# Banded attention of batches 2 and 3 in whole runs beside a channel mix, and a reordered last expert

## The chip, the cores and the metric

The kernel runs on one core of a Trainium2 chip. The metric is the device time of one execution in microseconds (us), the median of three runs. TensorE is called PE below, its weight loads PEld; VectorE is DVE, ScalarE is ACT, GpSimd is POOL, and SyncE (SP) issues most of the DMAs. Each engine works through its own list of instructions in order; a scheduler writes these lists when the kernel is built, from the order in which the code is written and from its priorities.

## The reference

Three layers on a batch of 4, sequence S = 576, width 512, all in float32:

```
q, k, v: (4, 8, 576, 64)                       # 8 heads of 64
1. banded attention: scores = q @ k.T / 8
   heads 0-3: 0 <= i-j < 32;  heads 4-7: 0 <= i-j < 128 and (i-j) % 4 == 0;  else -1e9
   x = softmax(scores) @ v                      -> (4, 576, 512)
2. channel mix: x_prev = x shifted by one row
   xk = mu_k*x + (1-mu_k)*x_prev;  xr = mu_r*x + (1-mu_r)*x_prev
   y = sigmoid(xr @ w_r) * (relu(xk @ w_k)**2 @ w_v)     # w_k 512x1024, w_v 1024x512
3. mixture of 4 attention experts: the gate picks the top 2 of y @ w_gate, with softmax weights
   out = sum over chosen e of weight_e * causal_attention_e(y) @ wo[e]   # head width 64
```

## The kernel before, in words

**Channel mix.** It is computed in half sequences of 288 columns. Every large product is made of three fp32r products (`product`, line 521): the high half of the weight with the high half of the data, high with low, and low with high. The halves of the data come from `mix`: ACT rounds the mixed data `m` to its high half `xh` (line 510), and POOL subtracts it to leave the low half `xl` (line 511). `receptance` makes `z`, `keys` makes `h` and splits its square into `kh` and `kl` (line 545, on DVE, for batch 1 on POOL for every second block), and `values_of` makes `v`. All these products use the whole 128 x 128 array.

**Banded attention.** Heads are taken in pairs, four pairs a batch. For each pair `attn_weights` makes scores for nine blocks of 64 queries, in two score buffers of five and four blocks; in each block the two heads (`j` = 0, 1) sit on two 64 x 64 tiles of the array (line 303). For batches 2 and 3 DVE and ACT then make the weights, DVE turns them in 32 x 32 squares (`turn_weights`), they go out to DRAM and come back as `pT`, and `attn_values` multiplies them by the values (line 377), again two small products per block. The attention of batch b+1 is issued beside the channel mix of batch b: `attn_batch` (batch 1) and `attn_later` (batches 2 and 3) are generators that a loop at the end advances together with the channel mix. From the written order the scheduler chooses, product by product, what PE does next.

**Expert attention.** For each batch and each pair of experts g, `queries_keys` makes `pq` and `pk`, splits them into `qh`, `ql`, `kh`, `kl` (lines 814 to 817, one buffer of each), and SP copies these into the operands `qs`, `kk`, `kl2` of the scores (line 823). `values` makes `pv` and the gate. `scores` (lines 910, 912) makes the causal scores of one expert in five blocks of queries and normalises them, `context` transposes the weights (`pt`, line 957), copies them (`wt`) and makes the value sums (`av`, lines 983, 988) of two experts together, and `project` makes the output (`po`, line 1020). A table `plan` says which generators go side by side with which expert, and in how many steps.

Of the kernel before, what the change touches and what calls it, by code (L numbers as in the profile page):

```python
# [21 lines left out]
def tile_dilated_attention__rwkv_channel_mix__moe_attention(  # L22
# [20 lines left out]
    DM = 512  # L43
# [237 lines left out]
    def attn_weights(ap, b, hp, qT, kT):  # L281
# [7 lines left out]
        def products(t0, t1):  # L289
# [67 lines left out]
    def attn_values(ap, b, hp, vw, pe=None, pT=None):  # L357
# [4 lines left out]
        for i in range(3):  # L362
# [69 lines left out]
    def attn_later(ap, first):  # L432
# [10 lines left out]
        for n, (b, hp) in enumerate(pairs):  # L443
# [9 lines left out]
            next(weights)  # L453
            if behind:
# [3 lines left out]
            yield  # L458
# [55 lines left out]
    def product(o, wts, xs, kts, wsl):  # L514
# [16 lines left out]
    def keys(dp, b, c, fo, kh, kl, xk, wts):  # L531
# [12 lines left out]
        half = nc.gpsimd if b == 1 and fo % 2 == 0 else nc.vector  # L544
# [191 lines left out]
    with s2:  # L736
# [61 lines left out]
        def queries_keys(b, g):  # L798
# [3 lines left out]
            ql = ep.tile([128, S], F32R, tag="ql", name=f"ql_{b}_{g}", bufs=1)  # L802
            kh = ep.tile([128, S], F32R, tag="kh", name=f"kh_{b}_{g}", bufs=1)
            qh = ep.tile([128, S], F32R, tag="qh", name=f"qh_{b}_{g}", bufs=1)
            kl = ep.tile([128, S], F32R, tag="kl", name=f"kl_{b}_{g}", bufs=1)
# [88 lines left out]
        def scores(b, e):  # L894
# [7 lines left out]
            for t, (t0, tn) in enumerate(TB):  # L902
# [3 lines left out]
                for i, (c0, c1) in enumerate(parts):  # L906
# [5 lines left out]
                    nc.tensor.matmul(sc, qs[g][:, e % 2, t0 : t0 + 128], kl2[g][:, e % 2, c0:c1],  # L912
                                     start=False, stop=True)
# [12 lines left out]
            nc.vector.tensor_scalar_add(st[:, 2, :], st[:, 2, :], 1e-9)  # L926
            nc.vector.reciprocal(st[:, 3, :], st[:, 2, :])
            assert ("v", b) in emitted
            nc.vector.tensor_mul(st[:, 3, :], st[:, 3, :], gt[:, :, e])
            for t, (t0, tn) in enumerate(TB):  # L930
                n = t0 + tn
                tn = 128
                pb = pe[:tn, PO[t] : PO[t] + n]
                if t == NB - 1:
                    nc.scalar.activation(pb, pb, AF.Copy, scale=st[:tn, 3, t : t + 1])
                else:
                    nc.vector.tensor_scalar_mul(pb, pb, st[:tn, 3, t : t + 1])
            weights[(b, e)] = pe
            yield
# [3 lines left out]
        def context(b, e):  # L943
# [5 lines left out]
            heads[e % 2] = []  # L949
            moved = []  # L950
            for i, grp in enumerate(groups):
                pt = ps("pt", f"pt2_{nm}_{i}")
                for kb, t in grp:
                    k0, kn = TB[kb]
                    tn = 128
                    c0 = place(kb, t)[1]
                    nc.tensor.transpose(pt[:kn, c0 : c0 + tn], pe[:tn, PO[t] + k0 : PO[t] + k0 + kn], ident[:tn, :tn])  # L957
                wt = ep.tile([128, 512], F32, tag="wt", name=f"wt{i}_{nm}", bufs=10)
                heads[e % 2].append(wt)
                for rows, c0, c1 in regions[i]:  # L960
                    if ("aava", "avav")[e % 2][i] == "a":
# [3 lines left out]
                yield  # L965
            if e % 2 == 0:
                return
            av1 = ps("av", f"av1_{nm}")
            av0 = ps("pt", f"av0_{nm}")
            two = [(64 * x, heads[x], vt[:, :, 64 * (2 * g + x) : 64 * (2 * g + x) + 64]) for x in range(2)]  # L970

            def after_all(ins):

                if kb == 0:
                    for m in moved:
                        tc.add_manual_dep(ins.ins, m.ins.name, together, reason="both experts' products together")

            for kb in range(NB):
                k0, kn = TB[kb]
                i, c0 = place(kb, max(kb, 1))  # L980
                q0 = max(k0, 64)
                for p0, w, vh in two:
                    ins = nc.tensor.matmul(av1[p0 : p0 + 64, q0 - 64 : 512], vh[:kn, kb, :], w[i][:kn, c0 : c0 + S - q0],  # L983
                                           start=(kb == 0), stop=(kb == NB - 1))
                    after_all(ins)
                if kb == 0:
                    for p0, w, vh in two:
# [121 lines left out]
```

## Time and profile before

| what | value |
|---|---|
| time, median of 3 runs | 571.47 us (571.39 to 571.98) |
| the profiled execution's own time, its span | 570.95 us, 569.2 us |
| PE busy | 548.3 us, 96% of the span |
| DVE, ACT, POOL busy | 349.9, 333.8, 64.8 us |
| granted TensorE clock, mean | 0.991 of full speed |
| 0 to 60 us | banded attention of batch 0, loading and splitting of the weights |
| 60 to 367 us | channel mix of batches 0 to 3, banded attention of batches 1 to 3 beside it |
| 367 to 569 us | expert attention |

How to read it: PE is busy nearly always, so the time is a sum of what PE does one after another, plus the stretches at the start, inside the expert attention and at the end in which it waits. A PE matmul's shown length includes the time in the pipeline, in which the next one already runs. What one costs is therefore the distance from its start to the next one's start. An fp32 product of the banded attention leaves two records in the trace, an fp32r product one.

### The profile page before, as it was taken

Reading aid. Unit: us, or ns where it says so; the run is one execution under the profiler, and the core shown is the slowest. Engines: PE = TensorE matmul, PEld = TensorE weight load, DVE = VectorE, ACT = ScalarE, POOL = GpSimd, SP = SyncE. Lnnn points to the kernel's source line nnn. Section 1 sums busy time; section 2 is a strip of 40 time slices with the busy share of each in tenths; the row PEclk is TensorE's granted clock in tenths of the full one; section 3 lists DMA queues with packets and bytes.
Section 4 is the critical chain, followed back from the end, with each engine's and each line's share of the span. In section 5 each row is a group of like instructions: output and inputs, shape, how many; then the busy total and the mean of one; then the engine's idle time right before and its main releaser. Section 6 shows DMA issues by size and latency. Waiting matters only on the chain.

```text
span 569.2 us, 12508 instructions
## 1 busy us (share of the span) xinstructions
PE 548.3 (96%) x4669; PEld 490.5 (86%) x4669; DVE 349.9 (61%) x1145; ACT 333.8 (59%) x940; POOL 64.8 (11%) x89
## 2 busy tenths in 40 slices
PE   9978989999999999999999999999998999999985
PEld 4757989989889999999999999999986988988663
DVE  3788989665889268356361526438667549565652
ACT  3789998655877075455253625227575757655851
POOL 8400000001123032110022303000000000000000
PEclk9997999999999999999999999999999999999998
DMA  9968296857676124120100320054504615506202
GB/s 165 244 209 244 85 243 126 146 100 164 136 162 147 43 60 119 40 52 27 38 1 1 83 67 1 2 126 115 137 23 103 171 30 126 139 24 181 76 0 94
DMA packets 130173, 57.66 MB, mean 101 GB/s; under 512 B 109928, under 2 KB 117184, under 8 KB 130112
## 3 DMA queue, kind: packets, MB, share of 16 engines
q1 hardware_dynamic: 129680, 56.41, 42.0%
q8 instruction: 37, 0.61, 0.5%
q0 software_dynamic: 416, 0.44, 0.4%
q14 instruction: 24, 0.20, 0.1%
q10 hardware_dynamic: 16, 0.00, 0.0%
HBM read 34.42 MB, written 10.03 MB: 78 GB/s over the span
## 4 chain that ended last, share of the span: by engine, by line
PE 81%; DVE 7%; ACT 5%; DMA 3%; SPq 2%; issue 1%; DVEq 0%; ACTq 0%
PE v L521 19%; PE h L521 14%; PE z L521 7%; PE pv L836 5%; PE sc L303 5%; PE av L983 5%; PE av L377 4%; PE po L1020 4%; PE pt L957 4%; PE pq L521 3%; PE pk L521 3%; PE idle L76 2%; PE sc L910 2%; PE sc L912 2%; SPq L189 2%; PE pt L367 2%
## 5 line engine op out<-in xcount | busy, mean ns | idle before, releaser
L521 PE MATMUL h<-xh,wk_hi 128*128 128x288 f32 x256 | 77.5, 304 | 1.8 <-ACT r L535 1.7
L521 PE MATMUL h<-xl,wk_hi 128*128 128x288 f32 x256 | 75.7, 296 | 0.6 <-DVE xl L500 0.6
L521 PE MATMUL v<-kh,wv_hi 128*128 128x288 f32 x256 | 75.7, 301 | 0.0
L521 PE MATMUL h<-xh,wk_lo 128*128 128x288 f32 x256 | 75.2, 294 | 0.0
L521 PE MATMUL v<-kl,wv_hi 128*128 128x288 f32 x256 | 75.1, 297 | 0.0
L521 PE MATMUL v<-kh,wv_lo 128*128 128x288 f32 x256 | 74.5, 295 | 0.0
L922 ACT ACTIVATE pe<-pe,st 128x64 f32<-128x64 f32 (+4 forms) x80 | 44.9, 562 | 19.2 <-DVE st L916 18.8
L535 ACT ACTIVATE r<-h 128x288 f32<-128x288 f32 x64 | 26.0, 410 | 48.6 <-PE h L521 42.4
L521 PEld LDWEIGHTS h<-xh,wk_hi 128*128 128x128 f32 x256 | 47.8, 187 | 4.5 <-ACT r L535 2.9
L511 POOL TENSOR_TENSOR xl<-m,xh 128x1152 fp32r<-128x1152 f32 x12 | 32.4, 2700 | 167.1 <-ACT xh L510 86.5
L916 DVE CUSTOM_DVE_ANT_0 pe<-sc,cmask 128x64 f32<-128x64 f32 (+4 forms) x80 | 33.6, 425 | 25.9 <-PE sc L912 25.7
L521 PEld LDWEIGHTS h<-xl,wk_hi 128*128 128x128 f32 x256 | 48.1, 188 | 0.9 <-DVE xl L500 0.8
L521 PEld LDWEIGHTS v<-kh,wv_hi 128*128 128x128 f32 x256 | 47.6, 187 | 1.2 <-DVE r L542 0.2
L521 PEld LDWEIGHTS h<-xh,wk_lo 128*128 128x128 f32 x256 | 48.2, 188 | 0.0
L521 PEld LDWEIGHTS v<-kh,wv_lo 128*128 128x128 f32 x256 | 47.9, 188 | 0.3
L521 PEld LDWEIGHTS v<-kl,wv_hi 128*128 128x128 f32 x256 | 47.9, 188 | 0.3
L327 ACT ACTIVATE pe<-pe,st 128x96 f32<-128x96 f32 x108 | 39.1, 365 | 13.4 <-DVE st L322 13.2
L497 DVE SCALAR_TENSOR_TENSOR m<-x,mus,m 128x288 f32<-128x288 f32 x64 | 29.9, 507 | 26.1 <-ACT m L496 26.1
L521 PE MATMUL z<-xh,wr_hi 128*128 128x288 f32 x128 | 39.8, 314 | 0.7 <-ACT z L529 0.7
L551 DVE SCALAR_TENSOR_TENSOR x<-z,v 128x288 f32<-128x288 f32 x32 | 14.3, 453 | 40.4 <-PE v L521 40.3
L521 PE MATMUL z<-xl,wr_hi 128*128 128x288 f32 x128 | 38.7, 303 | 0.0
L521 PE MATMUL z<-xh,wr_lo 128*128 128x288 f32 x128 | 38.2, 300 | 0.0
(183 smaller groups left out, 1439.2 us busy)
## 6 DMA issues: line engine op xcount, KB each, us to landing
kk<-kh SPq DMA_DIRECT2D x32, 144.0 KB, 2.7
kl<-kl SPq DMA_DIRECT2D x32, 144.0 KB, 2.6
raw_in_moe_w_k_dram<-in_moe_w_k_dram SPq DMA_DIRECT2D x4, 1024.0 KB, 7.5
raw_in_moe_w_v_dram<-in_moe_w_v_dram SPq DMA_DIRECT2D x4, 1024.0 KB, 6.4
out_dram<-ob SPq DMA_DIRECT2D x16, 256.0 KB, 3.1
rqk<-in_q_dram SPq DMA_DIRECT2D x48, 72.0 KB, 2.5
rqk<-in_k_dram SPq DMA_DIRECT2D x48, 72.0 KB, 2.5
moved<-turned SPq DMA_DIRECT2D x8, 432.0 KB, 2.9
```

The source lines that it names most:

```text
L303: nc.tensor.matmul(sc[h, c0 : c0 + WK], qT[h, QB * t : QB * t + QB], kT[h, k0 : k0 + WK], start=(b > 0), stop=(b > 0 or t == t1 - 1))
L327: nc.scalar.activation(pe[:, t, :], pe[:, t, :] if b else sc[:, c0 : c0 + WK], AF.Exp, bias=st[:, 0, t : t + 1], scale=-1.0, accum_out=st[ ...
L377: nc.tensor.matmul(av[64 * j : 64 * j + 64, p0 % 288 : p0 % 288 + u1 - u0], vw[:, j, t, :], (pts[:, 128 * a + 64 * j + u0 : 128 * a + 64 * ...
L497: nc.vector.scalar_tensor_tensor(out=m, in0=x, scalar=mus[:, 0, w, f : f + 1], in1=m, op0=ALU.mult, op1=ALU.add)
L511: nc.gpsimd.tensor_sub(lo, m, hi.bitcast(F32))
L521: nc.tensor.matmul(o, w[:, kt, wsl], x[:, kt, :], start=(n == 0), stop=(n == last))
L535: nc.scalar.activation(r, p, AF.Relu)
L836: nc.tensor.matmul(p, x[:, kt, t0 : t0 + tn], w[:, kt, 512:772], start=(n == 0), stop=(n == 3 * KT - 1))
L916: nc.vector.tensor_tensor_reduce(out=pe[:tn, PO[t] + c0 : PO[t] + c1], in0=sc, in1=m, scale=-0.125, scalar=(BIG if i == 0 else st[:tn, 1, ...
L922: nc.scalar.activation(pb, pb, AF.Exp, bias=st[:tn, 0, t : t + 1], scale=-1.0, accum_out=st[:tn, 2, t : t + 1])
L957: nc.tensor.transpose(pt[:kn, c0 : c0 + tn], pe[:tn, PO[t] + k0 : PO[t] + k0 + kn], ident[:tn, :tn])
L983: ins = nc.tensor.matmul(av1[p0 : p0 + 64, q0 - 64 : 512], vh[:kn, kb, :], w[i][:kn, c0 : c0 + S - q0], start=(kb == 0), stop=(kb == NB - 1))
```

## The change

It has five parts. (1) For batches 2 and 3 each couple of banded products (both heads of a block) is told to come after the latest channel-mix product that the code has issued so far (`together_with`). (2) In `mix` the high and low half are made in two pieces, of two of the four features each. (3) In batch 1 the low half of the seventh block of keys is made by DVE instead of POOL. (4) `ql`, `kh`, `qh`, `kl` have two buffers. (5) The last expert of the last batch has an order of its own: its scores are made from the last block of queries to the first and normalised in two groups, its weights are transposed in five groups, its value sums are made for the later 256 columns first, the last projection is split by g, three projections of batch 2 are held back to chosen places (`fill`), two of the last outputs are issued by ACT, and the last rows of the plan are other.

```diff
                 c0 = WK * (t - t0)
-                for j in range(2):
-                    h = slice(64 * j, 64 * j + 64)
-                    nc.tensor.matmul(sc[h, c0 : c0 + WK], qT[h, QB * t : QB * t + QB], kT[h, k0 : k0 + WK],
-                                     start=(b > 0), stop=(b > 0 or t == t1 - 1))
+                with together_with(b, 2):
+                    for j in range(2):
+                        h = slice(64 * j, 64 * j + 64)
+                        nc.tensor.matmul(sc[h, c0 : c0 + WK], qT[h, QB * t : QB * t + QB], kT[h, k0 : k0 + WK],
+                                         start=(b > 0), stop=(b > 0 or t == t1 - 1))
...
-                    for j in range(2):
-                        nc.tensor.matmul(
-                            av[64 * j : 64 * j + 64, p0 % 288 : p0 % 288 + u1 - u0],
-                            vw[:, j, t, :],
-                            (pts[:, 128 * a + 64 * j + u0 : 128 * a + 64 * j + u1] if pT is None
-                             else pT[:, 2 * j + u0 // 32 : 2 * j + u1 // 32, t, :]),
-                            start=True, stop=True,
-                        )
+                    with together_with(b, 2):
+                        for j in range(2):
+                            nc.tensor.matmul(
+                                av[64 * j : 64 * j + 64, p0 % 288 : p0 % 288 + u1 - u0],
+                                vw[:, j, t, :],
+                                (pts[:, 128 * a + 64 * j + u0 : 128 * a + 64 * j + u1] if pT is None
+                                 else pT[:, 2 * j + u0 // 32 : 2 * j + u1 // 32, t, :]),
+                                start=True, stop=True,
+                            )
...
         if b:
-            nc.scalar.copy(hi, m)
-            nc.gpsimd.tensor_sub(lo, m, hi.bitcast(F32))
+            for f in (slice(0, KT // 2), slice(KT // 2, KT)):
+                nc.scalar.copy(hi[:, f], m[:, f])
+                nc.gpsimd.tensor_sub(lo[:, f], m[:, f], hi[:, f].bitcast(F32))
...
-                nc.tensor.matmul(o, w[:, kt, wsl], x[:, kt, :], start=(n == 0), stop=(n == last))
+                marks["product"] = nc.tensor.matmul(o, w[:, kt, wsl], x[:, kt, :], start=(n == 0), stop=(n == last)).ins
...
+    def together_with(b, first):
...
+        return tc.issue_after(marks["product"]) if b >= first and "product" in marks else ExitStack()
...
-        half = nc.gpsimd if b == 1 and fo % 2 == 0 else nc.vector
+        half = nc.gpsimd if b == 1 and fo % 2 == 0 and fo < FT - 2 else nc.vector
...
-            ql = ep.tile([128, S], F32R, tag="ql", name=f"ql_{b}_{g}", bufs=1)
-            kh = ep.tile([128, S], F32R, tag="kh", name=f"kh_{b}_{g}", bufs=1)
...
+            ql = ep.tile([128, S], F32R, tag="ql", name=f"ql_{b}_{g}", bufs=2)
+            kh = ep.tile([128, S], F32R, tag="kh", name=f"kh_{b}_{g}", bufs=2)
...
-            for t, (t0, tn) in enumerate(TB):
+            for t in ([4, 3, 2, (3, 5), 1, 0, (0, 3)] if (b, e) == (B - 1, E - 1) else [*range(NB), (0, NB)]):
+                if isinstance(t, tuple):
+                    normalise(b, e, pe, *t)
...
+            if last:
+                turns = [[(1, 3), (1, 4), (2, 3), (2, 4)], [(3, 3), (3, 4), (4, 4)], [(0, 3), (0, 4)],
+                         [(1, 1), (1, 2), (2, 2)], [(0, 1), (0, 2), (0, 0)]]
+                for i, grp in enumerate(turns):
...
+                    if i == 2:
+                        yield from sums([1, 2, 3, 4, 0], 3, NB)
+                        keep(av1[:, 256:512], 320, S)
...
+                yield from sums([1, 0, 2], 1, 3)
+                keep(av0[:, 0:64], 0, 64)
+                keep(av1[:, 0:256], 64, 320)
...
+        fill = {(2, 2): "scores 322", (2, 3): "scores 324", (2, 4): "turn 31"}
...
+            order = [4, 3, 0, 1, 2] if last else range(b % 2 == 0, NB)
...
+                        queue = nc.scalar if last else nc.sync
...
-                (3, 1): [("c", 6), ("s", 6), ("p1", 3)],
-                (3, 2): [("c", 4), ("p2", 3), ("s", 6)],
-                (3, 3): [("c", 6), ("p2", 1)]}
+                (3, 1): [("c", 4), ("s", 6), ("p1", 3)],
+                (3, 2): [("s", 7), ("d", 6), ("c", 4), ("p2", 2)],
+                (3, 3): [("c", 3), ("p2", 2)]}
...
-        for b in range(B):
-            run(gens[f"p{b}"])
+        for what, n in (("p3", 2), ("c", 5), ("c", 1), ("c", 2), ("c", 3), ("c", 1), ("p3", 3), ("p3", 5)):
+            assert run(gens[what], n) or what == "p3", what
```

**The order on PE.** Between the channel mix's products of batch 1, before, the scores of the third pair of batch 2 (`sc_2_0`, `sc_2_5`: first block of the buffer in the name) stood like this; `z` are receptance products of both half sequences, and "x3" means three alike in a row:

```order
L521 MATMUL z_0_3_2162<-xh_0_4_1873,wr_lo 128x288
L303 MATMUL sc_2_0_2342<-kT_2_2279,qT_2_2277 64x96
L303 MATMUL sc_2_5_2353<-kT_2_2279,qT_2_2277 64x96
L521 MATMUL z_1_0_2203<-xh_1_5_1886,wr_hi 128x288
L303 MATMUL sc_2_5_2353<-kT_2_2279,qT_2_2277 64x96 x3
L521 MATMUL z_1_1_2228<-xh_1_5_1886,wr_hi 128x288
L303 MATMUL sc_2_5_2353<-kT_2_2279,qT_2_2277 64x96 x4
L521 MATMUL z_1_2_2249<-xh_1_5_1886,wr_hi 128x288
L521 MATMUL z_1_0_2203<-xl_1_5_1887,wr_hi 128x288
```

With the change the same scores stand like this, among the key products `h`:

```order
L524 MATMUL h_0_1_2330<-xl_0_6_2195,wk_hi 128x288
L524 MATMUL h_0_1_2330<-xh_0_6_2194,wk_lo 128x288
L304 MATMUL sc_2_0_2350<-kT_2_2285,qT_2_2283 64x96 x10
L304 MATMUL sc_2_5_2361<-kT_2_2285,qT_2_2283 64x96 x8
L524 MATMUL h_0_2_2370<-xh_0_6_2194,wk_hi 128x288
L524 MATMUL h_0_2_2370<-xl_0_6_2195,wk_hi 128x288
```

Nine of the pair's eighteen score products stood in one run and the other nine in three pieces of 2, 3 and 4; now the eighteen stand in one run. Over the stretch in which the banded products of batches 2 and 3 are mixed into the channel mix, they made 37 runs before and make 15 now: 7 of 18 score products and 8 of 20 value products.

**The order on ACT.** In the expert attention, where the queries and keys of batch 2 for g = 0 are split, before (the brackets are the semaphores that an instruction waits for; `qh` and `kh` are the copies in question):

```order
L814 CAST qh_0_5834<-pq_0_0_5836 128x288 [waits DMAHW0_49,DMAHW1_49,PE_49,Activation_49]
L922 ACTIVATE pe_1_0_5401,st_4762<-pe_1_0_5401,st_4762 128x320 [waits DVE_49]
L935 ACTIVATE pe_0_3_5278<-pe_0_3_5278,st_4763 128x576 [waits DVE_49,Activation_49]
L922 ACTIVATE pe_1_0_5401,st_4762<-pe_1_0_5401,st_4762 128x448 [waits DVE_49]
L816 CAST kh_0_5833<-pk_0_0_5837 128x288 [waits DMAHW6_49,DMAHW5_49,DMAHW7_49,DMAHW2_49,PE_49]
L962 COPY wt_0_3_5384<-pt_0_3_0_5379 64x512 [waits PE_49]
```

and with the change:

```order
L822 CAST qh_0_5858<-pq_0_0_5860 128x288 [waits DMAHW4_49,DMAHW3_49,PE_49]
L824 CAST kh_0_5857<-pk_0_0_5861 128x288 [waits DMAHW5_49,DMAHW2_49,DMAHW6_49,DMAHW1_49,PE_49]
L936 ACTIVATE pe_0_3_5302,st_4787<-pe_0_3_5302,st_4787 128x576 [waits DVE_49]
L936 ACTIVATE pe_1_0_5425,st_4786<-pe_1_0_5425,st_4786 128x64 [waits DVE_49,Activation_49]
L936 ACTIVATE pe_1_0_5425,st_4786<-pe_1_0_5425,st_4786 128x192 [waits DVE_49]
```

The copies still wait for DMAs, but for those that copied what the buffer held two groups of experts earlier, instead of one, and `kh` follows `qh` at once.

**The end on PE.** Before, the transposes of the last expert (`pt_3_3`), the value sums (`av_3_3`) and the last projection stood in three blocks:

```order
L957 MATMUL pt_3_3_2_7143<-ident,pe_3_3_7040 128x128 x4
L957 MATMUL pt_3_3_3_7150<-ident,pe_3_3_7040 128x128 x2
L957 MATMUL pt_3_3_3_7150<-ident,pe_3_3_7040 64x128
L983 MATMUL av_3_3_7157<-wt_3_2_7028,vt_6341 64x512
L983 MATMUL av_3_3_7157<-wt_3_3_7124,vt_6341 64x512
```

With the change two of the five groups of transposes and two finished output blocks' products (`po_4`, `po_3`) stand between the value sums:

```order
L975 MATMUL pt_3_3_3_7196<-ident,pe_3_3_7028 128x128 x3
L1009 MATMUL av_3_3_7136<-wt_3_2_7049,vt_6365 64x256
L1009 MATMUL av_3_3_7136<-wt_3_3_7174,vt_6365 64x256
L975 MATMUL pt_3_3_4_7202<-ident,pe_3_3_7028 64x128 x3
L1095 MATMUL po_4_7176<-woh,ctx_7125 128x512
L1095 MATMUL po_4_7176<-wol,ctx_7125 128x512
L1095 MATMUL po_3_7180<-woh,ctx_7125 128x512
L1095 MATMUL po_3_7180<-wol,ctx_7125 128x512
L1023 MATMUL av_3_3_7137<-wt_3_2_7122,vt_6365 64x64
```

The value sums of the first columns, which need the last transposes, now come behind projections instead of directly behind the transposes.

## Rows read from the trace of the kernel before

**Rows 1.** Windows view, all engines: busy us (records), clock, DMA share, GB/s.

```profile
136.20:285.20 149.00, 149.00 (x1429) 138.81 (x1428) 87.55 (x281) 80.46 (x255) 28.91 (x18) 1.00 0.37 88
170.00:180.00 10.00, 10.00 (x111) 9.12 (x112) 9.38 (x29) 6.62 (x23) 4.56 (x3) 1.00 0.74 167
427.00:436.00 9.00, 7.54 (x47) 5.59 (x48) 7.59 (x35) 6.01 (x17) 0.00 (x0) 1.00 0.66 159
536.00:558.00 22.00, 18.69 (x119) 12.98 (x119) 13.12 (x52) 13.71 (x37) 0.00 (x0) 1.00 0.08 30
```

**Rows 2.** Windows view of line 521 alone: PE busy, PEld busy, clock, DMA.

```profile
136.20:285.20 149.00, 123.57 (x857) 114.99 (x856) 1.00 0.37 88
```

**Rows 3.** Chain of waits: start us, us, what; 96 products in a row.

```profile
303.13 12.80 PE z L521 x96
```

**Rows 4.** PE's timeline: whole runs of banded products and what follows each.

```profile
94.29 1.70 PE L303 MATMUL sc<-kT,qT 64*64 64x96 f32 x36 [0.61 <-DVE kT L276]
95.93 0.40 PE L521 MATMUL v<-kh,wv_hi 128*128 128x288 f32 x1
...
212.55 1.39 PE L377 MATMUL av<-rqk,vw 96*64 96x64 f32 x40
213.86 0.40 PE L521 MATMUL v<-kh,wv_hi 128*128 128x288 f32 x1
```

**Rows 5.** PE's timeline: a pair's scores in pieces between products.

```profile
151.51 0.29 PE L521 MATMUL z<-xh,wr_lo 128*128 128x288 f32 x1
151.73 0.38 PE L303 MATMUL sc<-kT,qT 64*64 64x96 f32 x4
152.04 0.40 PE L521 MATMUL z<-xh,wr_hi 128*128 128x288 f32 x1
152.37 0.54 PE L303 MATMUL sc<-kT,qT 64*64 64x96 f32 x6
...
153.65 0.40 PE L521 MATMUL z<-xh,wr_hi 128*128 128x288 f32 x1
153.88 0.29 PE L521 MATMUL z<-xl,wr_hi 128*128 128x288 f32 x1
```

**Rows 6.** Timelines of ACT and POOL at the first mix; a POOL subtraction half as wide.

```profile
137.96 1.16 ACT L510 CAST xh<-m 128x1152 fp32r<-128x1152 f32 x1 [0.59 <-DVE m L497]
139.19 2.65 POOL L511 TENSOR_TENSOR xl<-m,xh 128x1152 fp32r<-128x1152 f32 x1 [52.92 <-ACT xh L510]
L746 POOL TENSOR_TENSOR yl<-x,yh 128x576 fp32r<-128x576 f32 x4 | 5.3, 1369 | 20.6 <-DVE x L551 20.6
```

**Rows 7.** ACT's first and last exponential of a pair; the turn; the way through DRAM (issues: KB each, us to landing).

```profile
142.17 0.37 ACT L327 ACTIVATE pe<-pe,st 128x96 f32<-128x96 f32 x1 [3.06 <-DVE st L322]
...
147.06 0.36 ACT L327 ACTIVATE pe<-pe,st 128x96 f32<-128x96 f32 x1
...
L348 DVE STREAM_TRANSPOSE turned<-pe 128x864 f32<-128x864 f32 x8 | 8.6, 1074 | 0.1
...
rqk<-moved SPq DMA_DIRECT2D x24, 144.0 KB, 3.7
moved<-turned SPq DMA_DIRECT2D x7, 432.0 KB, 2.6
```

**Rows 8.** Timelines of PE and ACT where queries and keys are split (last of four waits).

```profile
434.97 0.50 PE L1020 MATMUL po<-woh,ctx 128*128 128x512 f32 x1 [0.46 <-DVE kl L817]
...
432.39 0.40 ACT L816 CAST kh<-pk 128x288 fp32r<-128x288 f32 x1 [1.26 <-DMA kk<-kh]
```

**Rows 9.** PE's timeline in the last experts: three of its seven waits.

```profile
538.54 0.40 PE L910 MATMUL sc<-kk,qs 128*128 128x288 f32 x1 [0.39 <-DVE st L916]
...
553.26 1.19 PE L957 MATMUL pt<-ident,pe 128*64 128x128 f32 x8 [0.59 <-DVE pe L937]
...
556.62 1.07 PE L983 MATMUL av<-wt,vt 64*64 64x512 f32 x4 [0.73 <-DVE wt L964]
```

**Rows 10.** SP's timeline at the end: the last four output DMAs.

```profile
563.83 1.82 SPq L1028 DMA_DIRECT2D out_dram<-ob  x4
```

More of the change, by code (lines that the diff above doesn't have):

```diff
@@ L453, in attn_later @@
             next(weights)
+            yield
             if behind:
@@ L911, in scores @@
                                      start=True, stop=False)
-                    nc.tensor.matmul(sc, qs[g][:, e % 2, t0 : t0 + 128], kl2[g][:, e % 2, c0:c1],
-                                     start=False, stop=True)
+                    marks[f"scores {b}{e}{t}"] = nc.tensor.matmul(sc, qs[g][:, e % 2, t0 : t0 + 128], kl2[g][:, e % 2, c0:c1],
+                                                                  start=False, stop=True).ins
                     m = cmask[:tn, 448:512] if t == 0 else cmask[:, S - n + c0 : S - n + c1]
@@ L964, in context @@
                         moved.append(nc.vector.tensor_copy(wt[:rows, c0:c1], pt[:rows, c0:c1]))
-                yield
-            if e % 2 == 0:
-                return
+            if not last:
+                for i, grp in enumerate(groups):
+                    turn(i, [(kb, t, place(kb, t)[1]) for kb, t in grp], regions[i], ("aava", "avav")[e % 2][i])
+                    yield
+                if e % 2 == 0:
+                    return
             av1 = ps("av", f"av1_{nm}")
             av0 = ps("pt", f"av0_{nm}")
-            two = [(64 * x, heads[x], vt[:, :, 64 * (2 * g + x) : 64 * (2 * g + x) + 64]) for x in range(2)]
@@ L972, in after_all @@
[L972 to L987, printed above, removed]
-                        after_all(nc.tensor.matmul(av0[p0 : p0 + 64, 0:64], vh[:64, 0, :], w[3][:64, 256:320],
-                                                   start=True, stop=True))
@@ L990, in context, with spot, sums @@
-            yield
+            two = [(64 * x, x, vt[:, :, 64 * (2 * g + x) : 64 * (2 * g + x) + 64]) for x in range(2)]
+            def spot(x, kb, t):
+                i, c0 = places[kb, t] if last and x else place(kb, t)
+                return wts2[x][i], c0
+            def sums(blocks, ta, tz):
+                for kb in blocks:
+                    kn = TB[kb][1]
+                    t = max(kb, ta)
+                    q0, q1 = TB[t][0], TB[tz - 1][0] + 128
+                    for p0, x, vh in two:
+                        w, c0 = spot(x, kb, t)
+                        ins = nc.tensor.matmul(av1[p0 : p0 + 64, q0 - 64 : q1 - 64], vh[:kn, kb, :], w[:kn, c0 : c0 + q1 - q0],
+                                               start=(kb == blocks[0]), stop=(kb == blocks[-1]))
+                        if last:
+                            after(ins, [moved[places[kb, t][0]]])
+                        elif kb == 0:
+                            after(ins, moved)
+                    if kb == 0 and ta == 1:
+                        sums0()
+                    yield
@@ new lines, in sums0, with after, keep @@
+            def sums0():
+                for p0, x, vh in two:
+                    w, c0 = spot(x, 0, 0)
+                    after(nc.tensor.matmul(av0[p0 : p0 + 64, 0:64], vh[:64, 0, :], w[:64, c0 : c0 + 64],
+                                           start=True, stop=True), moved[-1:] if last else moved)
+            def after(ins, moves):
+                for m in moves:
+                    tc.add_manual_dep(ins.ins, m.ins.name, together, reason="both experts' products together")
+            def keep(src, c0, c1):
+                ch, cl = (ctxs[b][:, n, g, c0:c1] if c0 else heads_of[b // 2][:, n, g, 64 * (b % 2) : 64 * (b % 2) + 64]
+                          for n in range(2))
+                nc.scalar.copy(ch, src)
+                nc.vector.tensor_sub(cl, src, ch.bitcast(F32))
@@ L991, in context @@
+            if b < B - 1:
+                run(sums(range(NB), 1, NB))
+                yield
+            else:
+                yield from sums(range(NB), 1, NB)
             if g == 0:
@@ L994, in context @@
                     heads_of[b // 2] = ep.tile([128, 2, 2, 128], F32R, tag="c0", name=f"c0_{b}", bufs=2)
-            for src, c0, c1 in ((av0[:, 0:64], 0, 64), (av1, 64, S)):
-                ch, cl = (ctxs[b][:, n, g, c0:c1] if c0 else heads_of[b // 2][:, n, g, 64 * (b % 2) : 64 * (b % 2) + 64]
-                          for n in range(2))
-                nc.scalar.copy(ch, src)
-                nc.vector.tensor_sub(cl, src, ch.bitcast(F32))
+            keep(av0[:, 0:64], 0, 64)
+            keep(av1, 64, S)
             emitted.add(("c", b, g))
@@ L1075, in tile_dilated_attention__rwkv_channel_mix__moe_attention @@
                 merge(*[(part(gens[k], n), n) for k, n in plan[(b, e)]])
-        for b in range(B):
-            run(gens[f"p{b}"])
+        for what, n in (("p3", 2), ("c", 5), ("c", 1), ("c", 2), ("c", 3), ("c", 1), ("p3", 3), ("p3", 5)):
+            assert run(gens[what], n) or what == "p3", what
+        for g in gens.values():
+            assert not run(g, 1)
 _INS = ['q', 'k', 'v', 'moe_mu_k', 'moe_mu_r', 'moe_w_k', 'moe_w_v', 'moe_w_r',
```

121 lines of the change are left out of this document (73 added, 48 removed).

## The prediction

> **What bounds the kernel.** I read the windows first. In the stretch from 136.2 to 285.2 us, in which the banded products of batches 2 and 3 are mixed into the channel mix, PE is busy for all of its 149.00 us, while DVE has 87.55, ACT 80.46 and POOL 28.91 [rows 1]. The reader is to see that the clock is at its upper level throughout (1.00, that is 2.4 GHz), so neither waits nor clock can be gained there: only what PE does one after another counts. Next I took what one product costs where nothing is between: 96 take 12.80 us in the chain of waits, 0.1333 us each [rows 3], although each is shown with some 0.3 us. The stretch holds 856 of them [rows 2], so 114.1 us, and the other 34.9 us go to the banded products with all that their being mixed in costs. In the expert attention PE does wait: 1.46 us of the 9 us from 427 to 436, and 3.31 us of the 22 us from 536 to 558 [rows 1]. These two stretches and the banded products are where the change can act.
>
> **Banded products in whole runs.** A run of the 18 score products of a pair (36 records) takes 95.93 - 94.29 = 1.64 us to the next product's start, one of 20 value products (40 records) 213.86 - 212.55 = 1.31 us [rows 4]. Entering costs something: the last product ahead of a run takes 151.73 - 151.51 = 0.22 us, 0.09 more than usual; and so does leaving, where the first product behind takes 153.88 - 153.65 = 0.23 us, 0.10 more [rows 5]. A whole run thus costs 1.64 + 0.20 = 1.84 or 1.31 + 0.20 = 1.51 us. With the change the stretch has 7 of the one and 8 of the other: 12.9 + 12.1 = 25.0 us where 34.9 are spent now. That is 9.9 us less.
>
> To check this from the other side, I took one pair in pieces. Its second nine score products stand as 2, 3 and 4 with single products between, from 151.51 to 153.88, 2.37 us in all [rows 5]. Take off the four products at 0.1333 and 1.84 us are left, for half a pair, as much as a whole pair costs in one run. Two effects make it up. Each piece pays an entry and an exit; and a head alone costs almost what both do: a piece of three products (six records) is busy 0.54 us, one of two (four records) 0.38 [rows 5], so the third takes 0.16 us, where a whole run gives 1.64 / 9 = 0.18 us to a block of both heads. The two heads lie on different tiles and run side by side.
>
> Here the Trainium skill bears on the case. Its page "TensorEngine Tiling (Array Packing)", section "Key Properties", says that changing the tiling mode drains TensorE. By that rule alone the gain would be a fixed price for each switch saved, which is the first rival below; the 0.22 and 0.23 us above agree with it as far as they go, and the pieces of rows 5 cost more than that.
>
> **The mixes in halves.** When PE reaches the first mix of batch 1, it now does banded runs while POOL makes the low half. With the change the products of `z_0_0` come first and want it. ACT starts the high half at 137.96 and needs 1.16 us for all of it, so about 0.6 for a half; POOL needs 1.37 us for a half by a row of that width (2.65 for the whole) [rows 6]. The first half is there at about 137.96 + 0.6 + 1.37 = 139.9 to 140.1 us, and PE needs it with its second product, at about 140.0. I put 0.3 us of waiting (0 to 0.5). In one piece it would be there at 139.19 + 2.65 = 141.84 [rows 6], some 1.8 us late, so the halves are worth about 1.5 us to part 1. The later mixes and the one block of keys that goes from POOL to DVE I put at nothing: DVE is idle for 61 of the 149 us [rows 1] and PE has other products ahead of them.
>
> **The way of the weights.** The values need weights that pass ACT, DVE and DRAM. From a pair's first exponential (142.17) to the end of its last (147.06 + 0.36) are 5.3 us, with the mix's work between; the turn needs 1.07, the normalising is one more pass of DVE over the same weights, which I put at the same, the way out takes 2.6 and back 3.7 us [rows 7]: 13.7 us. In the new order a pair's values stand 106 to 120 products and one run of each kind behind its scores: 106 x 0.1333 + 1.84 + 1.51 = 17.5 us up to 19.4. I cost this wait at nothing, with about 4 us to spare; without that cover it is the last rival.
>
> **Two buffers for queries and keys.** ACT's `kh` stands 1.26 us for a DMA that copies the old `kh` out [rows 8]; behind it are the copies of transposed weights and the exponentials, and PE waits for them or for `kl`. With two buffers the awaited DMA belongs to the group before the last, long landed. From 427 to 436 PE idles 1.46 us in four waits [rows 1, 8]; each also costs the refill of PE's pipeline, about 0.15 us. 1.46 + 4 x 0.15 = 2.1; I take 2.0, between 0.8 (one wait goes, others stay) and 2.2.
>
> **The last expert.** From 536 to 558 PE idles 3.31 us [rows 1] in seven waits, for the score buffers (0.39), for normalised weights (0.59) and for copies of transposed weights (0.73) [rows 9]. With refills of about 0.17 they cost 4.5 us. With projections and value sums between the groups most go; but three groups of scores of expert 2 now stand back to back on two buffers, where one projection of 1.4 us was between, so one wait like that at 538.54 appears there; and two short ones stay at the transposes. I leave 1.8 us of waiting, and 0.4 for four more changes between transposes, value sums and projections: 4.5 - 1.8 - 0.4 = 2.3 us gained, between 0 (each wait comes back elsewhere) and 4.
>
> **The last outputs.** SP issues four DMAs in 1.82 us, 0.46 each, and only then can the last start [rows 10]. Now two blocks are finished some 2 us ahead of the others, and the last ones go from two queues. I take 0.7 us, one and a half issues, between 0 and 1.2. The Trainium skill ("DMA: Bandwidth & Descriptors", section "Issuing engines are not separate DMA queues") says that several issuing engines save only the time of issuing, since the same DMA engines carry it all. By that rule alone the second queue gives one issue, 0.46 us by the row, and the blocks' earlier end the rest.
>
> **The sum.** 9.9 - 0.3 + 2.0 + 2.3 + 0.7 = 14.6 us, against the profiled execution's own 570.95 us: 556.35. The median of the runs shown lies 0.52 us above that execution, so 556.9, and I say 556.8 us. At their best ends the terms give 9.9 + 2.2 + 4 + 1.2 = 17.3, which is 554.2.
>
> **The rivals.**
>
> Only the switches count. Then 22 runs fewer save 22 x 0.20 = 4.4 us instead of 9.9, the sum is 9.1, and the time 562.4. For it speaks that each of these prices is seen directly; against it that the 34.9 us don't come out without the second effect (15 whole runs and 22 x 0.2 make 29.4). 0.10.
>
> Only the banded runs gain. The waits in the expert attention move on: with two buffers DVE or the score buffers are late next (DVE has 7.59 of 9 us from 427 to 436 [rows 1]), and the end pays for its new switches. With 9.6 + 0.8 + 0 + 0.3 = 10.7 the time is 560.8. For it speaks how short each wait is, and that something else is late close behind. 0.17.
>
> The buffers and the tail make no difference and the runs are not kept together by the chip's real times: the order is fixed at build time and is read off above, so this has next to nothing, 0.02, at 571.5 us.
>
> The weights come late, and it is slower. PE works in order, so a values run whose `pT` is not back holds every product behind it; before, single pieces could stand anywhere. There are eight such runs. 14.6 us are used up when each waits 14.6 / 8 = 1.8 us, that is when the way takes 13.7 + 4 + 1.8 = 19.5 us. For it speaks that DVE, which masks the scores, normalises and turns, is busy 9.38 of 10 us from 170 to 180 with the DMA engines at 0.74 [rows 1]; against it that this is a short stretch, and that the way would have to be 6 us longer in all eight pairs. At 21 us each run waits 21 - 17.7 = 3.3 us, 26 us in all, and the time is 583. I give it 0.05, and 0.08 to a smaller part of it, with times from 559 to 570.
>
> **How the numbers follow.** The forecast's own case has 0.58, from 554 to 559.5. Its neighbours, the two rivals with partial gains, take the range up to 562.9; below 553.5 I see no row. The range 553.5 to 562.9 leaves out the slow cases and the worst of the partial one, together about 0.15. The measurement can tell about 0.2% from no change, 1.1 us. Faster by more than that is everything but the last rival's bad half and the case of no effect: 0.93; same 0.02; slower 0.05.
>
> **What would show it.** In the trace after: no run of one or two banded records in the stretch, 36 and 40 records in a run, and some 139 us from the first mix's products to where 149 are needed now. PE should show a wait of less than 0.5 us ahead of the first `z<-xl` and none ahead of value runs. ACT's `kh` should not wait for `kk<-kh`, and PE's idle time from 427 to 436 should mostly be gone. The last experts should keep under 2 us of idle PE, the largest at the scores of expert 2. The prediction is wrong if PE waits for `rqk<-moved` or POOL's `xl` at the runs, or if whole runs cost over 1.84 us.

## The result, and the profile after

| kernel | median | range | runs |
|---|---|---|---|
| before, measured again | 571.47 us | 571.39 to 572.80 | 5 |
| changed | 556.67 us | 556.35 to 556.97 | 5 |

The ratio is 0.9735, with a 95% interval from 0.9722 to 0.9748. The forecast was 556.8 us, its range 553.5 to 562.9. The profiled execution took 556.97 us, with a span of 555.2 us where the one before had 569.2: the 14.0 us are to be found in the trace.

The windows view of the changed kernel, all engines, in the stretch of the banded products, in the part of the expert attention that answers to 427 to 436 us before, and in the last experts (busy us, records, clock, DMA share, GB/s):

```profile
136.10:274.90 138.80, 138.80 (x1430) 134.96 (x1429) 87.30 (x283) 81.78 (x264) 28.31 (x24) 1.00 0.40 95
418.00:427.00 9.00, 7.97 (x51) 5.27 (x51) 6.96 (x31) 6.51 (x21) 0.00 (x0) 1.00 0.48 117
505.00:549.90 44.90, 43.73 (x275) 32.51 (x274) 25.91 (x100) 28.91 (x75) 0.00 (x0) 1.00 0.27 82
```

and the same view of the products' line alone:

```profile
136.10:274.90 138.80, 117.90 (x858) 114.39 (x857) 1.00 0.40 95
```

The first row answers to the first of [rows 1]: PE is still busy for all of it, at the same clock, with the same number of products and of records (one more at the window's edge), but it needs 138.8 us where it needed 149.0. The 857 products take 857 x 0.1333 = 114.2 us as before [rows 2, 3], so the banded products now cost 24.6 us instead of 34.9; the forecast's figure was 25.0. In the second row PE still idles 1.03 us of 9, where it idled 1.46: so it did not mostly go, as the prediction had it, and the wait at 424.03 below shows why. In the last row it idles 1.17 us in 45, where 22 us before held 3.31 [rows 1].

PE's timeline of the changed kernel shows the first mix, the first run of scores and the last run of values, and POOL's timeline the low half that the first mix needs:

```profile
139.87 0.29 PE L524 MATMUL z<-xh,wr_hi 128*128 128x288 f32 x1
140.00 0.29 PE L524 MATMUL z<-xl,wr_hi 128*128 128x288 f32 x1
140.13 0.29 PE L524 MATMUL z<-xh,wr_lo 128*128 128x288 f32 x1
...
142.93 0.29 PE L524 MATMUL z<-xh,wr_lo 128*128 128x288 f32 x1
143.15 1.70 PE L304 MATMUL sc<-kT,qT 64*64 64x96 f32 x36
144.78 0.40 PE L524 MATMUL z<-xh,wr_hi 128*128 128x288 f32 x1
...
273.58 1.39 PE L379 MATMUL av<-rqk,vw 96*64 96x64 f32 x40
274.90 0.40 PE L524 MATMUL h<-xh,wk_hi 128*128 128x288 f32 x1
...
138.64 1.43 POOL L514 TENSOR_TENSOR xl<-m,xh 128x576 fp32r<-128x576 f32 x1 [19.97 <-ACT xh L513]
```

The reader is to see that the runs cost what whole runs cost before [rows 4]: 144.78 - 143.15 = 1.63 us and 274.90 - 273.58 = 1.32 us, with the same 0.22 ahead (143.15 - 142.93). The low half was there just in time: its use starts at 140.00, 0.13 after the product before, without a wait (POOL's row, whose ends are rough, puts its end at 138.64 + 1.43 = 140.07); 0.3 us had been set aside for one.

These waits are left in the expert attention behind 423 us, and the output DMAs leave from two queues (PE's timeline, then the timelines of PE, ACT's and SP's queues at the end):

```profile
424.03 1.08 PE L1009 MATMUL av<-wt,vt 64*64 64x512 f32 x4 [0.73 <-DVE st L948]
...
513.15 1.07 PE L1009 MATMUL av<-wt,vt 64*64 64x512 f32 x4 [0.32 <-DVE wt L983]
...
521.25 0.36 PE L924 MATMUL sc<-kk,qs 128*128 128x192 f32 x1 [0.48 <-DVE st L930]
...
540.98 0.41 PE L975 MATMUL pt<-ident,pe 128*64 128x128 f32 x2 [0.35 <-ACT wt L981]
...
549.70 0.63 PE L1095 MATMUL po<-woh,ctx 128*128 128x512 f32 x2
550.75 0.37 ACTq L1108 DMA_DIRECT2D out_dram<-ob  x1
551.09 0.37 SPq L1108 DMA_DIRECT2D out_dram<-ob  x1
```

The one at 521.25 is the one that was foreseen, at the scores of expert 2 that stand back to back on two buffers. Those at 424.03 and 513.15 are new: value sums that did not wait in the kernel before now do.

### The profile page after: what moved, and what is told of

Read it like the earlier page. It is cut to its first block, busy times and chain, and to the rows that moved or that the text cites. A ratio compares the mean times of both kernels' runs of the same rounds, so it can differ in the third digit from the quotient of the medians.

```text
span 555.2 us, 12552 instructions
## 1 busy us (share of the span) xinstructions
PE 536.9 (97%) x4681; PEld 487.1 (88%) x4681; DVE 349.0 (63%) x1149; ACT 336.2 (61%) x955; POOL 64.4 (12%) x99
## 4 chain that ended last, share of the span: by engine, by line
PE 83%; DVE 5%; SPq 3%; DMA 3%; ACT 3%; issue 1%; DVEq 0%; ACTq 0%
PE v L524 19%; PE h L524 15%; PE z L524 8%; PE pv L844 5%; PE av L1009 5%; PE pt L975 5%; PE po L1095 4%; PE pq L524 4%; PE pk L524 4%; PE sc L304 4%; PE av L379 4%; PE sc L924 2%; PE sc L926 2%; DMA rqk<-in_k_dram 2%; SPq L189 2%; PE pt L368 1%
## 5 line engine op out<-in xcount | busy, mean ns | idle before, releaser
L514 POOL TENSOR_TENSOR xl<-m,xh 128x576 fp32r<-128x576 f32 x24 | 34.7, 1462 | 152.5 <-ACT xh L513 152.5
L553 DVE TENSOR_TENSOR kl<-r,kh 128x288 fp32r<-128x288 f32 x50 | 30.5, 614 | 15.6 <-ACT kh L551 15.5
```

The lines of the kernel that those rows point to most:

```text
L514: nc.gpsimd.tensor_sub(lo[:, f], m[:, f], hi[:, f].bitcast(F32))
L553: half.tensor_sub(kl[:, fo, :], r, kh[:, fo, :].bitcast(F32))
```

## The experiments

Two theories of the banded products stood against each other. By the first, a run costs more than its switches, because its first block hides nothing and a block whose heads stand apart is paid for twice. By the second, only entry and exit count, 0.20 us a run. The kernels also undo the other parts one by one. Each was timed against the kernel before; the ratio is to that one. Since an execution's opening stage, of which all orders are the same, does not end at the same time (the first receptance product of batch 1 started between 139.30 and 141.61 us), the last column gives the profiled span from that product on, less the changed kernel's 555.2 - 139.87 = 415.3 us.

| run | median | ratio (95% interval) | span from there |
|---|---|---|---|
| e1_no_pin | 564.75 | 0.9876 (0.9852 to 0.9900) | +7.5 |
| e5_heads_apart | 562.72 | 0.9841 (0.9814 to 0.9869) | +4.8 |
| e12_two_pieces | 558.79 | 0.9778 (0.9754 to 0.9801) | +2.1 |
| e2_whole_mix | 559.49 | 0.9786 (0.9763 to 0.9808) | +3.0 |
| e3_one_buffer | 558.61 | 0.9772 (0.9751 to 0.9792) | +2.1 |
| e4_old_tail | 558.45 | 0.9773 (0.9752 to 0.9794) | +1.8 |
| e6_out_on_sp | 557.48 | 0.9753 (0.9731 to 0.9774) | 0.0 |
| e9_fill_early | 557.09 | 0.9746 (0.9725 to 0.9766) | +0.2 |
| e7_keys_on_pool | 556.86 | 0.9748 (0.9733 to 0.9763) | 0.0 |
| e13_joined_late | 555.67 | 0.9728 (0.9712 to 0.9743) | -0.6 |
| e14_joined_early | 555.94 | 0.9730 (0.9715 to 0.9745) | -0.8 |

**Without the tie.** The change's own other parts stay.

```diff
-        return tc.issue_after(marks["product"]) if b >= first and "product" in marks else ExitStack()
+        return tc.issue_after(marks["product"]) if b > first + 1 and "product" in marks else ExitStack()
```

> The changed kernel with banded products of batches 2 and 3 no longer tied to the channel mix's last product; all else as changed. In the stretch they now stand in 33 runs instead of 15 and 13 blocks have their two heads apart. Theory (a run costs about 0.36 us besides its blocks: entry, exit and a first block that hides nothing; and a block whose heads are apart is paid twice, 0.16 us): 18 x 0.36 + 13 x 0.16 = 8.6 us more, about 565.2. Rival (only entry and exit count, 0.20 us a switch): 18 x 0.20 = 3.6 us more, about 560.3. Rival (the gain came from elsewhere, such as the halves of the mixes): no change, 556.7.

It took 8.1 us more, 7.5 by the span: near the 8.6 of the first theory and more than twice the 3.6 of the second. That the gain came from elsewhere is out. PE's timeline of this run shows a piece and what it costs:

```profile
151.70 0.29 PE L524 MATMUL z<-xh,wr_lo 128*128 128x288 f32 x1
151.92 0.71 PE L304 MATMUL sc<-kT,qT 64*64 64x96 f32 x12
152.56 0.40 PE L524 MATMUL z<-xh,wr_hi 128*128 128x288 f32 x1
```

Six score products, a third of a pair's eighteen, take 0.64 us, where a third of a whole run would be 0.54; with entry and exit it is 0.84.

**Two whole pieces.** The scores of a pair's five and four blocks are written a step apart.

```diff
-            for t0, t1 in ((0, 5), (5, 9)):
-                products(t0, t1)
+            products(0, 5)
+            yield
+            products(5, 9)
             yield
```

(One step less ahead of it keeps the count of steps.)

> The changed kernel with the scores of a pair written in two pieces, five blocks and four, a step apart: 21 runs instead of 15 in the stretch, every block still whole. Theory (0.36 us a run besides its blocks): 6 x 0.36 = 2.2 us more, about 558.9. Rival (0.20 us a switch): 1.2 us more, about 557.9. If a run of ten costs 0.97 us and one of eight 0.81, the two together cost 1.78 against 1.64 for the whole.

2.1 us more, in the median and in the span, for six runs more: 0.35 us a run. PE's timeline:

```profile
141.69 0.29 PE L526 MATMUL z<-xh,wr_lo 128*128 128x288 f32 x1
141.92 1.04 PE L304 MATMUL sc<-kT,qT 64*64 64x96 f32 x20
142.89 0.40 PE L526 MATMUL z<-xl,wr_hi 128*128 128x288 f32 x1
...
143.75 0.88 PE L304 MATMUL sc<-kT,qT 64*64 64x96 f32 x16
144.55 0.40 PE L526 MATMUL z<-xh,wr_hi 128*128 128x288 f32 x1
```

0.97 and 0.80 us are 1.77, where one run takes 1.63; with 0.20 for another entry and exit that is 0.34. So every run has some 0.15 us beyond the switches, which the second theory lacks.

**Heads apart.** Runs and places as in the changed kernel; within a run, one head's blocks come before the other's.

```diff
-            for t in range(t0, t1):
+            blocks = range(t0, t1)
+            for t, j in ([(t, j) for t in blocks for j in range(2)] if b < 2 else [(t, j) for j in range(2) for t in blocks]):
```

> The changed kernel with the same runs in the same places, but in a run of scores of batches 2 and 3 the five (or four) blocks of one head come first and then those of the other. No switch more or less. Theory (the two heads of a block run side by side, and apart each costs what both did): a run of 18 has 15 to 18 slots of 0.16 us instead of 9, 6 to 9 more in each of eight runs, 8 to 12 us more, about 565 to 569; a run takes 2.6 to 3.1 us instead of 1.64. Rival (only switches count): no change, 556.7, and 1.64 us.

```profile
144.67 0.29 PE L524 MATMUL z<-xh,wr_lo 128*128 128x288 f32 x1
144.89 2.36 PE L304 MATMUL sc<-kT,qT 64*64 64x96 f32 x36
147.18 0.40 PE L524 MATMUL z<-xh,wr_hi 128*128 128x288 f32 x1
```

The same 36 records take 147.18 - 144.89 = 2.29 us instead of 1.63. That the heads run side by side holds, and a switch explains none of it; but the price is 0.66 us a run, 7 x 0.66 = 4.6 us of the span's 4.8, against the 1.0 to 1.5 a run and the 8 to 12 us expected. A head alone within a long run costs 2.29 / 18 = 0.13 us, not 0.16. The Trainium skill ("TensorEngine Tiling (Array Packing)", "Key Properties") says that different tiles load and multiply in parallel; the run agrees that they overlap, by 0.66 of 2.29 us.

**Whole mixes.**

```diff
-            for f in (slice(0, KT // 2), slice(KT // 2, KT)):
+            for f in (slice(0, KT),):
```

> The changed kernel with high and low halves of a mix made in one piece each, as before. Prediction's reason: the low half of the first mix of batch 1 comes some 1.8 us after PE first wants it, and the halves are worth about 1.5 us: 558.2, with PE idle for POOL's xl near 140 us. Rival (the scheduler puts other products there, or the low half is early anyway): within 0.5 us of 556.7.

```profile
139.43 0.43 PE L524 MATMUL z<-xh,wr_hi 128*128 128x288 f32 x2
140.14 0.40 PE L524 MATMUL z<-xh,wr_hi 128*128 128x288 f32 x1 [0.28 <-DVE x L559]
141.38 0.40 PE L524 MATMUL z<-xl,wr_hi 128*128 128x288 f32 x1 [0.84 <-POOL x L124]
...
157.96 0.40 PE L524 MATMUL h<-xl,wk_hi 128*128 128x288 f32 x1 [0.33 <-POOL xl L514]
```

The scheduler pulled three products forward, and PE still stood until the low half was there: 141.38 - 139.43 - 3 x 0.1333 = 1.55 us, the 1.5 of the prediction. (The profile names POOL's memset behind it as releaser; POOL's subtraction ended at 138.69 + 2.64 = 141.33.) A later mix adds the wait at 157.96. From the first receptance product to 96 products near 292 us the run needs 2.3 us more; the rest of the 3.0 lies behind the start of the last product, in the end of the output, which took 6.1 us here and 5.2 to 5.3 in the other runs with the same end; why is open.

**One buffer of queries and keys.**

```diff
-            ql = ep.tile([128, S], F32R, tag="ql", name=f"ql_{b}_{g}", bufs=2)
-            kh = ep.tile([128, S], F32R, tag="kh", name=f"kh_{b}_{g}", bufs=2)
+            ql = ep.tile([128, S], F32R, tag="ql", name=f"ql_{b}_{g}", bufs=1)
+            kh = ep.tile([128, S], F32R, tag="kh", name=f"kh_{b}_{g}", bufs=1)
```

(`qh` and `kl` likewise.)

> The changed kernel with one buffer each of ql, kh, qh and kl, as before. The two traces put the gain between the first gate values and the last value sums of batch 2 at 2.4 us, of which 1.4 us are six projection products that now stand behind that point. Theory from the traces (the buffers are worth the rest): 1.0 us more, 557.7, and ACT's kh waits for kk<-kh again. The prediction's term: 2.0 us more, 558.7. Rival (the order around, not the buffers, removed the waits): 556.7.

The waits of [rows 8] are back: here a window of the run, ACT's timeline and PE's.

```profile
418.00:426.90 8.90, 6.86 (x42) 4.27 (x43) 6.70 (x30) 6.23 (x18) 0.00 (x0) 1.00 0.49 116
...
421.83 0.40 ACT L824 CAST kh<-pk 128x288 fp32r<-128x288 f32 x1 [1.35 <-DMA kk<-kh]
...
424.80 0.50 PE L1095 MATMUL po<-woh,ctx 128*128 128x512 f32 x1 [0.85 <-DVE kl L825]
```

The run takes 2.0 us more: the prediction's term. The figure of 1.0 that I had read off the two traces was wrong. It compared the times at one landmark, the last value sums of batch 2, and took off 1.4 us for projection products moved behind it, at the price of six of them in a row; but where the order differs such a subtraction does not separate the parts.

**The old end.** The kernel before, with parts 1 to 4 alone.

> The kernel before with parts 1 to 4 of the change, and the last expert, the projections and the end as before. Theory from the traces (tail 2.1 us, end 0.45 us): 2.6 us more than the changed kernel, 559.3, and the seven waits between the last experts stand again. The prediction's terms: 3.0 us more, 559.7. Rival (seen without the moved products the tail gained only 0.7 us, and the end 0.45): 557.8.

All seven waits stand again, as in [rows 9]; three of them in PE's timeline:

```profile
526.30 0.40 PE L918 MATMUL sc<-kk,qs 128*128 128x288 f32 x1 [0.39 <-DVE st L924]
...
541.01 1.19 PE L965 MATMUL pt<-ident,pe 128*64 128x128 f32 x8 [0.59 <-DVE pe L945]
...
544.37 1.08 PE L991 MATMUL av<-wt,vt 64*64 64x512 f32 x4 [0.73 <-DVE wt L972]
```

The new end is worth 1.8 us, by the median and by the span, less than the prediction's 3.0. The buffers' 2.0 and this 1.8 make the 3.7 us that remain of 14.0 after the banded stretch's 10.3, to 0.1.

**Outputs on SP alone.**

```diff
-                        queue = nc.scalar if last else nc.sync
+                        queue = nc.sync
```

> The changed kernel with all output DMAs issued by SP. Theory (two issues on one queue stand one behind the other): about 0.4 us more, 557.1, with the last issue 0.4 us later. Rival (the DMAs' own time covers it, or the two blocks are not ready at once): no change, 556.7.

```profile
550.24 0.63 PE L1095 MATMUL po<-woh,ctx 128*128 128x512 f32 x2
...
551.46 1.02 SPq L1108 DMA_DIRECT2D out_dram<-ob  x2
```

From the start of these two last products the run ends after 555.7 - 550.24 = 5.5 us, the changed kernel after 555.2 - 549.70 = 5.5 us, though SP now issues two in a row where each queue had one. The second queue brings nothing that can be seen here. The median's 0.8 us more is in no part of the profile behind the opening stage, in which this execution lost 0.5.

**A projection earlier.**

```diff
-        fill = {(2, 2): "scores 322", (2, 3): "scores 324", (2, 4): "turn 31"}
+        fill = {(2, 2): "scores 320", (2, 3): "scores 324", (2, 4): "turn 31"}
```

> The changed kernel with the projection po_2 of batch 2 held behind the first group of scores of the last batch's expert 2 instead of the third, so that it stands between groups that share two score buffers. Theory (the one wait of 0.48 us for a score buffer at the changed kernel's 521.25 goes): 0.4 to 0.6 us less, 556.2. Rival (the wait only moves to the next group, or DVE is late in any order): no change, 556.7.

The wait at the second group of scores is gone, yet no time is saved. PE's timeline of this run, behind the projection:

```profile
522.39 0.33 PE L924 MATMUL sc<-kk,qs 128*128 128x320 f32 x1
522.56 0.31 PE L926 MATMUL sc<-kl,qs 128*128 128x320 f32 x1
523.01 0.47 PE L924 MATMUL sc<-kk,qs 128*128 128x448 f32 x1
```

The products at 522.56 last 0.45 us to the next start, some 0.28 more than the one before them: the group after next is held up instead, as it seems for the same two buffers, and transposes further on take some of the rest (those at 523.99 last 1.10 us to the next start, the changed kernel's at 523.95 0.91). The rival was right.

**Keys on POOL.**

```diff
-        half = nc.gpsimd if b == 1 and fo % 2 == 0 and fo < FT - 2 else nc.vector
+        half = nc.gpsimd if b == 1 and fo % 2 == 0 else nc.vector
```

> The changed kernel with the low half of the seventh block of keys of batch 1 on POOL again. The prediction put this part at nothing: 556.7. Rival (POOL's longer subtraction makes the value products of batch 1 wait): up to 0.6 us more for the two half sequences, 557.3.

No change, as the prediction had put it.

**Scores and values in one run.** The prices above say that 7 of the 15 runs can be saved. In the first of two kernels the scores are written a step later, in the second the value sums a step earlier:

```diff
             weights = attn_weights(ap, b, hp, qT, kT)
             next(weights)
-            yield
             if behind:
                 run_out(behind)
             if n + 1 < len(pairs):
                 vw[n + 1] = load_v(ap, *pairs[n + 1])
+            yield
             next(weights)
```

(This is the second; in the first the `yield` goes ahead of `weights`.)

> The changed kernel with the scores of a pair written one step later, directly ahead of the value sums of the pair before, so that both stand in one run of 38: 8 runs instead of 15 in the stretch. Theory (a run costs 0.20 us of entry and exit and up to 0.16 in its first block): 7 x 0.20 to 7 x 0.35, 1.4 to 2.4 us less, 554.3 to 555.3. Rival (the weights come late: between a pair's scores and its values stand only some 98 products, 13.1 us, where the way of the weights was put at 13.7 us): PE waits for rqk<-moved at the runs by about 1 us each, 7 us in all, some 562.

> The same run of 38, but with the value sums written one step earlier, directly behind the scores of the next pair, as the code before had it. Theory: 1.4 to 2.4 us less, 554.3 to 555.3. Rival: the weights come late, as in the run with the scores written later; some 562.

Both are a little faster than the changed kernel, 0.6 to 0.8 us by the span and 0.7 to 1.0 by the median, though the intervals of their ratios overlap with that of the changed kernel; that is less than the 1.4 to 2.4 expected. PE's timeline of the second, at the first joined run and at one that waits, and of the first at its only wait:

```profile
143.21 0.29 PE L524 MATMUL z<-xh,wr_lo 128*128 128x288 f32 x1
143.43 1.70 PE L304 MATMUL sc<-kT,qT 64*64 64x96 f32 x36
145.06 1.39 PE L379 MATMUL av<-rqk,vw 96*64 96x64 f32 x40
146.37 0.40 PE L524 MATMUL z<-xh,wr_hi 128*128 128x288 f32 x1
...
191.30 1.70 PE L304 MATMUL sc<-kT,qT 64*64 64x96 f32 x36
193.43 1.39 PE L379 MATMUL av<-rqk,vw 96*64 96x64 f32 x40 [0.42 <-ACT pe L328]
...
239.63 0.29 PE L524 MATMUL h<-xh,wk_lo 128*128 128x288 f32 x1
240.35 0.40 PE L524 MATMUL h<-xh,wk_hi 128*128 128x288 f32 x1 [0.42 <-DVE r L550]
```

Within a joined run scores still take 1.63 and values 1.31 us: just one entry and exit is saved, 7 x 0.20 = 1.4 us, not the 0.15 beyond. Each kernel gives some of that back in one wait. In the second, the values at 193.43 come 2.13 us after the scores' start instead of 1.63; the profile names an exponential as releaser, but the last `rqk<-moved` had landed only at 193.23. In the first no values wait, but the key product at 240.35 comes 0.72 us after the one ahead of it, where 0.13 is usual, held by DVE. So the way of the weights becomes the bound, as the rival said, but in one pair of seven of one kernel, and not in all.

The second kernel also undoes a line of the change that is not among its five parts: the changed code writes a pair's value sums one step later than the code before did (this `yield`). By this run the change is no better for it.

## Why the prediction was right

The mechanisms that the sum rests on were there, but that it met the median to 0.2 us is in part luck: the banded term came out 0.7 us larger than forecast, and the last expert with the outputs 1.2 us smaller.

**Banded products in whole runs: shown, and 0.7 us better.** Forecast 9.9 - 0.3 us, measured 10.3: the two traces agree to 0.1 us ahead of the stretch (the last value product ahead of the first mix starts at 139.74, before at 139.81) and the products behind it start 10.4 us earlier (274.90 against 285.29). The count of runs, 37 to 15, and the prices of [rows 4, 5] gave it. Undoing the tie alone takes back 7.5 us, in 33 runs; the other 2.8 us lie in what the rest of the change did to the order (37 runs before; the halves of the mixes and the moved `yield` act there too), which was not taken apart further. The prices found do add up, as an estimate: by the places where runs break off in the traces, 19 blocks had their heads in different runs before, 13 without the tie and none in the changed kernel. With 0.35 us a run (two pieces) and 0.07 (0.66 / 9, heads apart) to 0.16 us [rows 5] for such a block, 22 runs and 19 blocks make 9.0 to 10.7 us, where 10.3 were measured, and 18 runs and 13 blocks 7.2 to 8.4, where it was 7.5. The halves of the mixes are needed for the gain: without them 2.3 us come back, more than the 1.5 put on them, since a later mix, which was put at nothing, waits too. The 0.3 us set aside for the first mix were not needed, since the low half's first piece came as PE reached it.

**Why a run costs what it does: the direction held, one size did not.** That the switches alone (0.20 us) are not the price is shown by the two-piece kernel, 0.35 us a run. That heads apart cost twice is too much: in a long run they cost 0.66 us in 1.63. The forecast did not rest on it, as the sum came from 34.9 us measured whole.

**Two buffers: right in size, one sign not borne out.** 2.0 us forecast, 2.0 measured by the kernel with one. PE's waits for `kl` and `ql` are gone, and ACT's `kh` starts at 417.03, 0.30 us behind `qh`, without a wait. But PE's idle time did not mostly go, as the prediction had it: 1.03 us are left of 1.46, 0.73 of them the new wait at 424.03. That the size came out all the same has some luck in it: a wait of 0.34 us for `kl<-kl` at 399.08, outside the window that the sum went by, went too (it is back at 388.36 with one buffer).

**The last expert and the outputs: right in kind, over-estimated.** Forecast 2.3 + 0.7, measured 1.8 together. One term that was mis-sized is the end, 0.7: the second queue is worth nothing, by the kernel without it. From the start of the last product to the end of the span is 5.3 us in the changed kernel (a product behind 549.70) and 5.4 in the one with the old end, so nearly all of the 1.8 lies ahead of that point, against a term of 2.3. The waits there went about as forecast: seven with 3.30 us of idle PE in the kernel with the old end, three with 1.15 in the changed one, which with the prediction's 0.17 for each refill is 2.8 us. So the new order's own cost was set too low: it took some 1.1 us, as what is left over, where 0.4 had been set. The Trainium skill's rule ("DMA: Bandwidth & Descriptors", "Issuing engines are not separate DMA queues") had a second queue save the time of issuing and no more; in this case even that does not show, with 5.5 us to the end either way.

**The rivals.** Weights that come late cost nothing in the changed kernel: there is no row of PE's waits from 130 to 290 us. Where the margin was taken away, by joining, one wait appeared in one of two kernels. In the four pairs for which the trace has the last landing of `rqk<-moved`, the way took 11.4 to 16.9 us from the end of the scores, where 13.7 had been put from the first exponential; it was back at least 2.6 us ahead of the values, where about 4 had been counted on. That only the switches count would have given 4.4 us in the banded stretch, where 10.3 were measured; that only the banded runs gain is out by the 2.0 and 1.8 us of the buffers and the end.

## What to carry to other kernels

When an engine is busy all the time, price a change by the distance from start to start of whole runs in its timeline, and count the runs in the built order: that gave 25.0 us where 24.6 were measured. Small products on tiles of the array belong in whole runs, with partners on different tiles next to each other; what feeds the first product behind such a run must then be early, or be cut in pieces, since the run no longer fills its wait. Don't split a gain between parts by landmarks in two traces whose order differs; build the kernel with one part undone.

## What the runs showed of the hardware

- Between products of the full array, entering and leaving a run of tile products costs 0.20 us together, and the run some 0.15 us more, whatever its length: 10 score products take 0.97 us, 8 take 0.80, 18 take 1.63.
- In a run of 64 x 64 score products with 96 x 64 value products right behind them, both take what they take apart (1.63 and 1.31 us). That saves the 0.20 us of going to the full array and back, but not the 0.15; whether this is a price of going from the one kind of tile to the other is not shown.
- Score products on one tile one after the other take 0.13 us each in a long run, where two on different tiles take 0.18 together.
- The second queue for the last outputs changed the end by less than 0.1 us (5.5 us both ways, in one trace each).
